# One bank of each visit of maxima goes to ScalarE, and most of those banks hold the difference of two key blocks

## The chip, the cores and the metric

The kernel runs on one core of a Trainium2 chip. The metric is the device time of one execution in microseconds. Besides the times of several runs there is one execution recorded by the hardware profiler. Its engines are called PE (TensorE matmul) and PEld (its weight loads), DVE (VectorE), ACT (ScalarE), POOL (GpSimd) and SP (SyncE, which issues the transfers).

## The reference

Two attentions over the same 2048 tokens of width 448 (16 heads of 28) are mixed with a gate per token. Branch A is linear attention on learned features; branch B is plain softmax attention.

```python
g = _sigmoid((x * gate_w).sum(-1, keepdims=True))
a = _A_ref(x, A_wqkv, A_w_phi, A_wo)
b = _B_ref(x, B_wqkv, B_wo)
return g * a + (1 - g) * b
# in _B_ref
scores = jnp.einsum("bhqd,bhkd->bhqk", q, k) * scale
p = _softmax(scores, axis=-1)
o = jnp.einsum("bhqk,bhkd->bhqd", p, v)
```

The softmax of branch B subtracts the largest score of each query and head. The kernel finds those largest scores in a pass of its own, and this pass is what the change is about.

## The kernel before

**Names.** Heads are taken four at a time: `g` is one of four groups of heads. Queries are taken 512 at a time (`qb`, four blocks), and `gq` counts the 16 pairs of group and query block. Keys are taken 512 at a time where maxima are sought (`kb`, four blocks) and 128 at a time where probabilities are computed (`kt`, 16 tiles).

**Stages.** The front stage projects queries and keys and writes them to HBM (`qkd`), runs branch A, and projects the values. Between its matmuls it already seeks maxima for the first query blocks in 76 units (`mx_unit`, lines 242 to 279). A unit does two heads at once: half of its rows hold the difference of two key blocks. ScalarE takes the relu of that difference (line 270), and VectorE adds it to the score of the other block and takes the maximum in the same instruction (line 272); max(a, b) = b + relu(a - b).

**The late stage** is one loop over 256 steps (lines 1063 to 1101). Step `s` belongs to one `gq` and one key tile `kt`, so 16 steps make one `gq`. Each step does, in this order:

- `scores(s, 0)` and `scores(s, 1)`: four matmuls, one for each head, into four PSUM banks (`st`, line 821), and for each bank an exp on ScalarE into an SBUF tile (`p`, line 839).
- `values(s - 1)`: the probabilities of the step before times the values, into one bank held for the whole `gq` (`pv`, line 947).
- Once in 16 steps `finish`: `pv` is copied out, 384 columns by VectorE and then 128 by ScalarE (line 369). Normalization follows in the next steps, with transfers of the denominators (lines 372, 383, 384), a product on GpSimd (line 390) and a cast on ScalarE (line 398).
- `mx_visit` (lines 287 to 312) in the first 180 steps: the maxima of one tile of 128 queries against one key block for the four heads of a group. Four matmuls that work on 28 rows each go to four banks (`pm`, line 302), and VectorE reduces each bank to a column of `part` (line 306). When a `gq` is finished, `mx_reduce` reduces its columns, negates and transposes them into `nm`, from which the maxima are loaded later as a row of the queries (line 807). The visits run well ahead of the steps that need them: they begin with the last query tile of `gq` 4 in step 1.

**Order.** PE, DVE, ACT and POOL run their instructions in the order in which this program writes them. For SP a scheduler decides the order. The order of the visits is the list `flats`: key block outermost, then query tile.

**Banks.** Seven PSUM banks, `g0` to `g6`, are handed around by the lists `free`, `used` and `held`; the eighth is `pv`. In a step the four scores take four banks, and the visit takes four: the banks of its first and second score of this step and two that the last visit used. The first bank of a visit goes back to `free` at once (line 888), and the next step's fourth score takes it. That score must wait until the bank has been read. The fourth bank of a visit is taken by the third score two steps later.

**Loads.** `mx_load` (line 180) brings the keys of four heads, one block, into a tile `kc` with one transfer per head; there are five such buffers. `mx_query` brings the queries (`qc`). When the group changes (twice in the late stage), the tiles of the next group are loaded as the blocks of the old one are used for the last time (line 307).

Of the kernel before, what the change touches and what calls it, by code (L numbers as in the profile page):

```python
# [8 lines left out]
F32 = mybir.dt.float32  # L9
# [30 lines left out]
def gated_mix_kernel(ctx, tc, xT, wqkB, wvB, wvA, wkAT, wqAT, phi, woA, woB,  # L40
# [116 lines left out]
    acts = []  # L157
    subs = []
    part = mxp.tile([P, NU * 4], F32, name="part", bufs=1)
    neg = mxp.tile([P, 32], F32R, name="neg", bufs=1)  # L160
    nc.vector.memset(f32(neg), 0.0)

# [8 lines left out]
    def mx_rows(r, rows, src, heads, c):  # L171

        for i, j in zip(rows, heads):
            nc.sync.dma_start(f32(r[32 * i:32 * i + DH]), src[DH * j:DH * j + DH, 0, c:c + 512])
        return r

    def mx_tile(tag, nm, bufs):
        return mxp.tile([P, 512], F32R, tag=tag, name=nm, bufs=bufs)

    def mx_load(g, c):  # L180
        mxs[("kc", g, c)] = mx_rows(mx_tile("kc", f"kc{g}_{c}", 5), range(4), k_d[g], range(4),
                                    c * 512)

    def mx_query(gq):
        g, qb = divmod(gq, NQ)
# [2 lines left out]
    def pair_load(g, c):  # L188

        hp, b = divmod(c, 2)  # L190
        heads = (2 * hp, 2 * hp + 1)
        r = mx_tile("kc", f"kp{g}_{c}", 5)
        t = front.tile([P, 512], F32R, tag="kt", name=f"kt{g}_{c}", bufs=1)
        mx_rows(r, (0, 1), k_d[g], heads, b * 1024)
        mx_rows(r, (2, 3), k_d[g], heads, b * 1024 + 512)
        mx_rows(t, (2, 3), k_d[g], heads, b * 1024)
        mxs[("kp", g, c)] = r

        def sub():
            for i in (2, 3):  # L200
                js = slice(32 * i, 32 * i + DH)
                nc.gpsimd.tensor_sub(r[js], f32(r[js]), f32(t[js]))

        subs.append(sub)
# [37 lines left out]
    def mx_unit():  # L242

        u = mxs["u"]
        if u == NF:
            return
        mx_fin()
        mxs["u"] = u + 1
        gq, r = divmod(u, 16)
        g, qb = divmod(gq, NQ)  # L250
        if gq < GM:
            c, qt = divmod(r, 4)
            hp, b = divmod(c, 2)
            col = 64 * gq + 16 * b + 4 * qt + 2 * hp
            if r in (4, 9):
                pair_query(gq + 1, r // 9)
        else:
            c, qt = divmod(r, QM)
            hp, b = divmod(c, 2)
            col = 64 * gq + 4 * QM * b + 4 * qt + 2 * hp  # L260
            if r == 0:
                mx_query(gq)
        qc, kc = mxs[("qp", gq, hp)], mxs[("kp", g, c)]
        pb, pd = ps_mx(f"pmb{u}", False), ps_mx(f"pmd{u}", True)
        for j in range(4):
            js = slice(32 * j, 32 * j + DH)
            nc.tensor.matmul((pb if j < 2 else pd)[:, j % 2, :], qc[js, qt * P:(qt + 1) * P],  # L267
                             kc[js, :], start=True, stop=True, tile_position=(32 * j, 0))
        rl = rlp.tile([P, 2, 512], F32, tag="rl", name=f"rl{u}", bufs=2 if psn[1] == 3 else 1)
        nc.scalar.activation(rl, pd, AF.Relu)  # L270
        for i in range(2):
            nc.vector.tensor_tensor_reduce(rl[:, i, :], pb[:, i, :], rl[:, i, :], 1.0, LOWEST,  # L272
                                           ALU.add, ALU.max, part[:, col + i:col + i + 1])
        if gq < GM and qt == 3 and qb == NQ - 1:
            pair_load(g + 1, c)
        if gq == GM and qt == QM - 1:
            mx_load(g, c)
        if r == 15:
            mx_reduce(gq)


    flats = [(GM, kb, qt, h, 64 * GM + 8 * QM + 4 * (4 - QM) * kb + 4 * (qt - QM) + h)
             for kb in range(4) for qt in range(QM, 4) for h in range(4)]
    flats += [(gq, kb, qt, h, 64 * gq + 16 * kb + 4 * qt + h) for gq in range(GM + 1, NG * NQ)
              for kb in range(4) for qt in range(4) for h in range(4)]

    def mx_visit():

        fins = mxs["fin"][:]
        mxs["fin"].clear()  # L290
        f = mxs["f"]
        todo = flats[f:f + 4]
        mxs["f"] = f + len(todo)
        if todo:
            gq, kb, qt, _, col = todo[0]
            g, qb = divmod(gq, NQ)
            if kb == 1 and qt in (0, QM) and gq + 1 < NG * NQ and ("qc", gq + 1) not in mxs:
                mx_query(gq + 1)
            pm = mx_banks(f)
            for j in range(4):  # L300
                js = slice(32 * j, 32 * j + DH)
                nc.tensor.matmul(pm[j], mxs[("qc", gq)][js, qt * P:(qt + 1) * P],  # L302
                                 mxs[("kc", g, kb)][js, :], start=True, stop=True,
                                 tile_position=(32 * j, 0))
            for j in range(4):
                nc.vector.tensor_reduce(part[:, col + j:col + j + 1], pm[j], AX.X, ALU.max)  # L306
            if qt == 3 and qb == NQ - 1 and g + 1 < NG:
                mx_load(g + 1, kb)
            if qt == 3 and kb == 3:
                mx_reduce(gq)  # L310
        for fn in fins:
            fn()
# [502 lines left out]
    def scores(s, i):  # L815

        gq, kt = divmod(s, NT)
        g, qb = divmod(gq, NQ)

        def score(j, st):  # L820
            nc.tensor.matmul(st, kst_of[(g, kt // 4)][:, j, (kt % 4) * P:(kt % 4 + 1) * P],  # L821
                             qst_of[gq][:, j, :], start=True, stop=True)

        if s == 0:
            p = at.tile([P, 2, 512], F32, name=f"p{s}_{i}")
            st = ps_mx(f"st{s}_{i}", i)
            for jl in range(2):
                score(2 * i + jl, st[:, jl, :])
            nc.scalar.activation(p, st, AF.Exp, scale=SCALE)
            pts.setdefault(s, []).extend([p[:, 0, :], p[:, 1, :]])  # L830
            return
        sts = []
        for j in (2 * i, 2 * i + 1):
            used.append(free.pop(0))
            sts.append(bank(used[-1], f"st{s}_{j}"))
            score(j, sts[-1])
        for st in sts:
            p = late_p.tile([P, 512], F32, tag="p", name=f"p{s}_{len(pts.get(s, []))}", bufs=12)
            nc.scalar.activation(p, st, AF.Exp, scale=SCALE)  # L839
# [330 lines left out]
```

## Time and profile before

| | us |
|---|---|
| median of 3 runs | 1059.6 |
| lowest and highest | 1058.47 to 1061.05 |
| the profiled execution, whole | 1062.47 |
| its span in the trace | 1060.4 |
| visits: first and last maxima matmul | 364.2 to 853.9 |

The profile has several views. The page gives busy time for each engine and 40 equal slices of the span, in which each digit is the busy share in tenths. The view by stretches repeats the busy time for chosen parts, with the number of instructions in brackets. The view by lines groups instructions: busy time, mean duration of one in nanoseconds, and idle time ahead of them with its cause. For one line it gives counts with shortest, median and longest duration. The view in order of time gives start, duration, engine, line, operation, tiles and count, and in square brackets the idle time of the engine just before, with what ended it; several instructions of one kind in a row are merged. The list of waits gives who waited for whom: total, times, longest. The chain of waits follows the work that ended last back from its end.

### The profile page before, as it was taken

Reading aid. Unit: us, or ns where it says so; the run is one execution under the profiler, and the core shown is the slowest. Engines: PE = TensorE matmul, PEld = TensorE weight load, DVE = VectorE, ACT = ScalarE, POOL = GpSimd, SP = SyncE. Lnnn points to the kernel's source line nnn. Section 1 sums busy time; section 2 is a strip of 40 time slices with the busy share of each in tenths; the row PEclk is TensorE's granted clock in tenths of the full one; section 3 lists DMA queues with packets and bytes.
Section 4 is the critical chain, followed back from the end, with each engine's and each line's share of the span. In section 5 each row is a group of like instructions: output and inputs, shape, how many; then the busy total and the mean of one; then the engine's idle time right before and its main releaser. Section 6 shows DMA issues by size and latency. Waiting matters only on the chain.

```text
span 1060.4 us, 17608 instructions
## 1 busy us (share of the span) xinstructions
PE 1046.2 (99%) x6344; PEld 559.5 (53%) x6344; DVE 727.2 (69%) x1351; ACT 756.3 (71%) x1388; POOL 227.8 (21%) x189
## 2 busy tenths in 40 slices
PE   8999999999999999999999999999999999999998
PEld 7777777778777633333333333333333333353545
DVE  5476677897745699999999999999999930000102
ACT  5455565587755777877777777777777798969682
POOL 1234454688536400110000000000000000000000
PEclk9999999999999999999999999999999999999999
DMA  8973100122333822223441233442242234405311
GB/s 290 300 227 96 50 30 30 41 79 78 95 109 100 183 57 55 62 59 84 107 95 48 58 76 97 127 103 60 52 99 50 53 83 96 118 32 149 101 58 53
DMA packets 64190, 99.08 MB, mean 93 GB/s; under 512 B 18008, under 2 KB 24776, under 8 KB 64104
## 3 DMA queue, kind: packets, MB, share of 16 engines
q1 hardware_dynamic: 64104, 97.97, 33.8%
q8 instruction: 50, 0.82, 0.3%
q14 instruction: 36, 0.29, 0.1%
HBM read 69.77 MB, written 27.78 MB: 92 GB/s over the span
## 4 chain that ended last, share of the span: by engine, by line
PE 87%; DVE 7%; DMA 2%; ACT 1%; SPq 1%; issue 1%; POOL 0%; ACTq 0%; DVEq 0%; POOLq 0%
PE st L821 26%; PE pv L947 21%; PE pm L302 7%; PE pqk L108 6%; PE pk L126 4%; PE poa L108 3%; PE pva L126 3%; DVE part L306 3%; PE pob L108 3%; PE pmb L267 3%; PE pq L108 2%; PE pvb L126 2%; PE pvb L108 1%; PE pn L503 1%; PE pqk L605 1%; DMA kst<-qkd 1%
## 5 line engine op out<-in xcount | busy, mean ns | idle before, releaser
L839 ACT ACTIVATE p<-st 128x512 f32<-128x512 f32 x1020 | 526.0, 607 | 137.9 <-PE st L821 134.7
L306 DVE TENSOR_REDUCE part<-pm 128x1 f32<-128x512 f32 x720 | 446.7, 683 | 36.1 <-PE pm L302 35.4
L821 PE MATMUL st<-qst,kst 128*128 128x512 f32 x1024 | 334.7, 439 | 5.0 <-DMA qst<-nm 1.9
L947 PE MATMUL pv<-p,vb 128*32 128x512 f32 x2048 | 273.4, 606 | 0.0
L821 PEld LDWEIGHTS st<-qst,kst 128*128 128x128 f32 x1024 | 173.7, 188 | 175.5 <-DVE part L306 61.7
L272 DVE CUSTOM_DVE_ANT_0 rl<-pmb,rl 128x512 f32<-128x512 f32 x152 | 98.2, 684 | 53.9 <-ACT rl L270 53.9
L390 POOL TENSOR_TENSOR oUb<-oUb,rsb 128x512 f32<-128x512 f32 x15 | 19.3, 1285 | 518.3 <-DMA rsb<-rdb 240.9
L302 PEld LDWEIGHTS pm<-kc,qc 28*128 28x128 f32 x720 | 34.4, 181 | 150.9 <-ACT p L839 150.1
L270 ACT ACTIVATE rl<-pmd 128x1024 f32<-128x1024 f32 x76 | 78.1, 1028 | 39.2 <-PE pmd L267 31.3
L302 PE MATMUL pm<-kc,qc 28*128 28x512 f32 x720 | 90.9, 495 | 0.0
L947 PEld LDWEIGHTS pv<-p,vb 128*32 128x32 f32 x2048 | 40.3, 108 | 72.1 <-issue 66.9
L958 DVE SCALAR_TENSOR_TENSOR acc<-pob,gate,acc 128x448 f32<-128x448 f32 x12 | 8.2, 684 | 94.4 <-PE pob L108 94.4
L108 PE MATMUL pqk<-XH,wB 128*128 128x512 f32 x192 | 59.6, 397 | 1.4 <-DVE ev L543 1.4
L369 DVE COPY oUb<-pv 128x384 f32<-128x384 f32 x15 | 8.3, 551 | 68.9 <-PE pv L947 68.9
L108 PE MATMUL poa<-woA_s,oTa 128*128 128x448 f32 x192 | 43.4, 375 | 0.0
L542 ACT CAST ev<-pqk 128x512 fp32r<-128x512 f32 x28 | 16.0, 588 | 35.5 <-PE pqk L108 34.4
L108 PEld LDWEIGHTS pqk<-XH,wB 128*128 128x128 f32 x192 | 35.3, 188 | 10.2 <-DVE ev L543 1.8
L126 PE MATMUL pk<-wkA_s,XH 128*128 128x448 f32 x128 | 39.4, 381 | 0.0
L267 PE MATMUL pmd<-kp,qp 28*128 28x512 f32 x152 | 37.9, 494 | 1.3 <-DVE part L272 1.3
L108 PEld LDWEIGHTS poa<-woA_s,oTa 128*128 128x128 f32 x192 | 34.9, 188 | 6.3 <-issue 3.3
L267 PE MATMUL pmb<-kp,qp 28*128 28x512 f32 x152 | 38.0, 496 | 0.0
L126 PE MATMUL pva<-wvA_s,XH 128*128 128x450 f32 x128 | 37.8, 371 | 0.0
(151 smaller groups left out, 1102.7 us busy)
## 6 DMA issues: line engine op xcount, KB each, us to landing
qkd<-ev SPq DMA_DIRECT2D x28, 512.0 KB
qst<-qkd SPq DMA_DIRECT2D x64, 224.0 KB
kst<-qkd SPq DMA_DIRECT2D x64, 224.0 KB
od<-oTb SPq DMA_DIRECT2D x48, 112.0 KB
rsa<-rda SPq DMA_DIRECT2D x8, 512.0 KB
rsb<-rdb SPq DMA_DIRECT2D x15, 256.0 KB
gad<-ga SPq DMA_DIRECT2D x16, 224.0 KB
acc<-gad SPq DMA_DIRECT2D x4, 896.0 KB
```

The lines of the kernel that those rows point to most:

```text
L108: nc.tensor.matmul(dst, l, r, start=i == 0, stop=i == len(todo) - 1)
L126: nc.tensor.matmul(dst[:, :n], l, r, start=i == 0, stop=i == len(todo) - 1, skip_group_check=True)
L267: nc.tensor.matmul((pb if j < 2 else pd)[:, j % 2, :], qc[js, qt * P:(qt + 1) * P], kc[js, :], start=True, stop=True, tile_position=(32 * ...
L270: nc.scalar.activation(rl, pd, AF.Relu)
L272: nc.vector.tensor_tensor_reduce(rl[:, i, :], pb[:, i, :], rl[:, i, :], 1.0, LOWEST, ALU.add, ALU.max, part[:, col + i:col + i + 1])
L302: nc.tensor.matmul(pm[j], mxs[("qc", gq)][js, qt * P:(qt + 1) * P], mxs[("kc", g, kb)][js, :], start=True, stop=True, tile_position=(32 * ...
L306: nc.vector.tensor_reduce(part[:, col + j:col + j + 1], pm[j], AX.X, ALU.max)
L390: (nc.gpsimd if n == 1 else nc.vector).tensor_mul(oU, oU, rs)
L542: nc.scalar.copy(e[:, 0, :], pq)
L821: nc.tensor.matmul(st, kst_of[(g, kt // 4)][:, j, (kt % 4) * P:(kt % 4 + 1) * P], qst_of[gq][:, j, :], start=True, stop=True)
L839: nc.scalar.activation(p, st, AF.Exp, scale=SCALE)
L947: nc.tensor.matmul(pv[32 * j:32 * j + 32, :], vb[kt // 8][:, kt % 8, 4 * g + j, :], pt[j], start=kt == 0, stop=kt == NT - 1, tile_position ...
```

## The change

In the late stage one of the four banks of each visit is read by ScalarE instead of VectorE. In visit `kb` this is the bank of head `kb`, and it is the first one: its matmul is issued first and it lies in the bank that goes to the next step's fourth score.

For heads 0, 1 and 2 that bank holds a difference: the tile of keys for block `c` has, in the rows of head `c`, the keys of block `c + 1` less those of block `c`, and in the rows of head `c - 1` those of block `c - 1`. GpSimd makes the difference (`diffs`, three subtractions per group, with the subtrahends in a further tile `kd`; `take_diffs` queues each subtraction two visits after its load was issued). ScalarE writes the relu of the difference into a tile `rl`. In the next visit VectorE adds it to the bank that holds block `c` of that head and takes the maximum in one instruction, as the units do. For head 3 in visit 3 ScalarE copies the bank, and VectorE reduces the copy at the end of the next visit. So four visits have nine reductions of banks, three joins and one reduction of a copy, where they had sixteen reductions. `part` is first filled with a very low number, since some of its columns stay unwritten.

With it go: key blocks innermost in the order of visits; loads of the next group's tiles in the last five visits of the old group; nine buffers of `p` instead of twelve; `kt`, a tile of the front stage, in the place of `kd`.

```diff
+    nc.gpsimd.memset(part, LOWEST)
...
     def mx_load(g, c):
+        mxs[("kc", g, c)] = r = mx_tile("kc", f"kc{g}_{c}", 5)
+        if c == 0:
+            mxs["kd"] = mx_tile("kd", f"kd{g}", 1)
+            for h in range(3):
+                mx_rows(mxs["kd"], (h,), k_d[g], (h,), h * 512)
+        for h in range(4):
+            mx_rows(r, (h,), k_d[g], (h,), 512 * (c + (c == h and c < 3) - (c == h + 1 and c > 0)))
+        if c < 3:
+            js, t = slice(32 * c, 32 * c + DH), mxs["kd"]
+            diffs.append((mxs["u"] + mxs["f"] // 4, lambda: nc.gpsimd.tensor_sub(
+                r[js], f32(r[js]), f32(t[js]))))
+
+    def take_diffs(n):
+        while diffs and diffs[0][0] + n <= mxs["u"] + mxs["f"] // 4:
+            diffs.pop(0)[1]()
...
-             for kb in range(4) for qt in range(QM, 4) for h in range(4)]
+             for qt in range(QM, 4) for kb in range(4) for h in range(4)]
...
     def mx_visit():
+        take_diffs(2)
...
-            pm = mx_banks(f)
-            for j in range(4):
+            pm = mx_banks(f, kb)
+            for j in sorted(range(4), key=lambda j: j != kb):
...
-            for j in range(4):
-                nc.vector.tensor_reduce(part[:, col + j:col + j + 1], pm[j], AX.X, ALU.max)
-            if qt == 3 and qb == NQ - 1 and g + 1 < NG:
-                mx_load(g + 1, kb)
+            rl = late_p.tile([P, 512], F32, tag="rl", name=f"rl{f}", bufs=2)
+            nc.scalar.activation(rl, pm[kb], AF.Relu if kb < 3 else AF.Copy)
+            for j in sorted({0, 1, 2, 3} - {kb}, key=lambda j: j == kb - 1):
+                if j == kb - 1:
+                    r = mxs["rl"]
+                    nc.vector.tensor_tensor_reduce(r, pm[j], r, 1.0, LOWEST, ALU.add, ALU.max,
+                                                   part[:, col + j:col + j + 1])
+                else:
+                    nc.vector.tensor_reduce(part[:, col + j:col + j + 1], pm[j], AX.X, ALU.max)
+            mxs["rl"] = rl
+            if kb == 3:
+                mxs["fin"].append(lambda: nc.vector.tensor_reduce(
+                    part[:, col + 3:col + 4], rl, AX.X, ALU.max))
+            if qb == NQ - 1 and g + 1 < NG:
+                if qt == 2 and kb == 3:
+                    mx_load(g + 1, 0)
+                if qt == 3 and kb < 3:
+                    mx_load(g + 1, kb + 1)
...
-    def mx_banks(f):
+    def mx_banks(f, first):
         b = [free.pop(0) for _ in range(4)]
         free.append(b[0])
         held.extend(b[1:])
-        return [bank(i, f"pm{f}_{j}") for j, i in enumerate(b)]
+        order = [first] + sorted({0, 1, 2, 3} - {first}, key=lambda j: j == first - 1)
+        return [bank(b[order.index(j)], f"pm{f}_{j}") for j in range(4)]
```

More of the change, by code (lines that the diff above doesn't have):

```diff
@@ L178, in mx_tile @@
         return mxp.tile([P, 512], F32R, tag=tag, name=nm, bufs=bufs)
+    diffs = []
     def mx_load(g, c):
-        mxs[("kc", g, c)] = mx_rows(mx_tile("kc", f"kc{g}_{c}", 5), range(4), k_d[g], range(4),
-                                    c * 512)
+        mxs[("kc", g, c)] = r = mx_tile("kc", f"kc{g}_{c}", 5)
[12 more added lines that the diff above has]
+            diffs.pop(0)[1]()
     def mx_query(gq):
@@ L192, in pair_load @@
         r = mx_tile("kc", f"kp{g}_{c}", 5)
-        t = front.tile([P, 512], F32R, tag="kt", name=f"kt{g}_{c}", bufs=1)
+        t = mx_tile("kd", f"kt{g}_{c}", 1)
         mx_rows(r, (0, 1), k_d[g], heads, b * 1024)
@@ L282, in gated_mix_kernel @@
     flats = [(GM, kb, qt, h, 64 * GM + 8 * QM + 4 * (4 - QM) * kb + 4 * (qt - QM) + h)
-             for kb in range(4) for qt in range(QM, 4) for h in range(4)]
+             for qt in range(QM, 4) for kb in range(4) for h in range(4)]
     flats += [(gq, kb, qt, h, 64 * gq + 16 * kb + 4 * qt + h) for gq in range(GM + 1, NG * NQ)
-              for kb in range(4) for qt in range(4) for h in range(4)]
+              for qt in range(4) for kb in range(4) for h in range(4)]
     def mx_visit():
+        take_diffs(2)
         fins = mxs["fin"][:]
@@ L837, in scores @@
         for st in sts:
-            p = late_p.tile([P, 512], F32, tag="p", name=f"p{s}_{len(pts.get(s, []))}", bufs=12)
+            p = late_p.tile([P, 512], F32, tag="p", name=f"p{s}_{len(pts.get(s, []))}", bufs=9)
             nc.scalar.activation(p, st, AF.Exp, scale=SCALE)
```

## The prediction

> **What bounds the kernel now.** I read the page first: its busy shares, and the slices of VectorE and ScalarE.
>
> ```profile
> span 1060.4 us, 17608 instructions
> PE 1046.2 (99%) x6344; PEld 559.5 (53%) x6344; DVE 727.2 (69%) x1351; ACT 756.3 (71%) x1388; POOL 227.8 (21%) x189
> DVE  5476677897745699999999999999999930000102
> ACT  5455565587755777877777777777777798969682
> ```
>
> TensorE's 99% says little, since a matmul that waits counts as busy. The second row of digits matters: from about 365 to 854 us VectorE is at nine tenths. That is the stage of the 180 visits, and the change acts in it alone. The view by stretches compares it with steps that have no visit:
>
> ```profile
> core 0: us, PE busy (x) PEld busy (x) DVE busy (x) ACT busy (x) POOL busy (x), PEclk, DMA share, GB/s
> 364.00:854.00 490.00, 486.84 (x2872) 182.81 (x2868) 455.21 (x771) 379.10 (x744) 30.84 (x25) 1.00 0.31 76
> 857.00:875.00 18.00, 18.00 (x104) 7.08 (x106) 0.57 (x3) 17.58 (x35) 2.58 (x2) 1.00 0.44 97
> ```
>
> 490 us for 180 steps is 2.72 us a step; VectorE works 455 of them (93%), ScalarE 379 (77%). VectorE is nearly full, but not full, so I asked for one step in order of time:
>
> ```profile
> 651.96 0.50 PE L302 MATMUL pm<-kc,qc 28*128 28x512 f32 x4
> ...
> 652.39 1.36 PE L821 MATMUL st<-qst,kst 128*128 128x512 f32 x4
> ...
> 652.49 2.48 DVE L306 TENSOR_REDUCE part<-pm 128x1 f32<-128x512 f32 x4 [0.22 <-PE pm L302]
> 652.92 2.06 ACT L839 ACTIVATE p<-st 128x512 f32<-128x512 f32 x4 [0.62 <-PE st L821]
> 653.24 0.19 PEld L821 LDWEIGHTS st<-qst,kst 128*128 128x128 f32 x1 [0.33 <-DVE part L306]
> ...
> 653.68 1.06 PE L947 MATMUL pv<-p,vb 128*32 128x512 f32 x8
> ...
> 654.68 0.51 PE L302 MATMUL pm<-kc,qc 28*128 28x512 f32 x4
> ...
> 655.21 1.29 DVE L306 TENSOR_REDUCE part<-pm 128x1 f32<-128x512 f32 x2 [0.23 <-PE pm L302]
> ...
> 655.65 0.60 ACT L839 ACTIVATE p<-st 128x512 f32<-128x512 f32 x1 [0.66 <-PE st L821]
> ```
>
> Here is a ring. The bank of the visit's first maxima is given to the fourth score of the next step. VectorE starts on it at 652.49; the fourth score's weights load at 653.24 (+0.75), pv starts at 653.68 (+0.44), the next maxima at 654.68 (+1.00), VectorE on them at 655.21 (+0.53): 2.72 us, the step. So VectorE's *first* reduction sits in the ring, and the other three do not: VectorE idles 0.22 us a step, and ScalarE idles 0.62 at the very place where the ring passes it. The list of waits counts the ring's wait once a visit, and the steps without visits give TensorE's own pace:
>
> ```profile
> PEld st L821 <- DVE part L306: 61.7, 180, 0.8
> ...
> 873.55 1.19 PE L821 MATMUL st<-qst,kst 128*128 128x512 f32 x4
> ...
> 874.68 1.06 PE L947 MATMUL pv<-p,vb 128*32 128x512 f32 x8
> ```
>
> Unstalled, four scores take 1.13 us to pv, against 1.29 in the visit step. TensorE's floor for a visit step is then 1.13 + 1.00 + 0.43 (maxima to scores, 651.96 to 652.39) = 2.56 us.
>
> **The change, part by part.** *The ring.* The bank that goes to the fourth score is now the one that ScalarE reads. In place of VectorE's first reduction stands one ACTIVATE. The single instructions:
>
> ```profile
> 619.62 0.69 DVE L306 TENSOR_REDUCE part<-pm 128x1 f32<-128x512 f32 x1 [0.23 <-PE pm L302]
> L270 ACT ACTIVATE rl<-pmd 128x1024 f32<-128x1024 f32 x76 | 78.1, 1028 | 39.2 <-PE pmd L267 31.3 <-ACT z_s L456 2.5 <-ACT vb L665 1.7
> L398 ACT CAST oTb<-oUb 128x512 fp32r<-128x512 f32 x15 | 9.6, 642 | 0.0
> ```
>
> The reduction takes 0.69, which leaves 0.06 of the 0.75 for the signal. No relu of 128x512 stands in the trace. Below: half of L270's relu, 0.51. Above: the cast of that size, 0.64, or no better than the reduction, 0.69. I take the ScalarE row that follows an idle engine and reads one bank of the same size, the 0.60 at 655.65, and the same 0.06. The ring loses 0.09: 180 x 0.09 = 16.2 us, or 1.44 per 16 steps. At 0.51 TensorE's floor decides, 2.72 - 2.56 = 0.16 a step, 29 us; at 0.69 nothing is gained here.
>
> *Does ScalarE have room?* It queues the relu behind the step's four exps and ahead of the next four. Four exps take 2.06 with the last at about 0.60, so each starts 0.49 behind the one before; five need 2.43 of the new 2.63. The exps end at 652.92 + 2.06 = 654.98, before the maxima at 655.21; the relu fills the idle 0.62 and the next exp starts behind it (655.21 + 0.49 = 655.70, against 655.65 now). Room is left: 0.20 a step.
>
> *VectorE.* Of four reductions a visit, 13 instructions in four visits remain: nine reductions, three joins, one reduction of a stored bank. A join is what L272 does now, and its accumulator read stands beside the next instruction:
>
> ```profile
> L272 DVE CUSTOM_DVE_ANT_0 rl<-pmb,rl 128x512 f32<-128x512 f32 x152 | 98.2, 684 | 53.9 <-ACT rl L270 53.9
> L272 DVE DVE_READ_ACCUMULATOR2_ANT part<- 128x1 f32 x152 | 12.6, 83 | 0.0
> ```
>
> The visit's work falls from 2.48 to about 1.9 (2.5 in one of four), under the step and out of the ring: its banks are wanted a step later. A relu may overwrite its buffer only when VectorE has read it. In the one visit of four with the stored bank that read ends 2.48 and a signal of 0.06 after the step's maxima came, and the relu wants the buffer at 2.63: nothing, and 0.1 x 45 = 4 us if that read takes 0.2 more.
>
> *What happens once in 16 steps.* Two steps in 16 are long now, because VectorE also copies pv (L369) or reduces the finished columns (L232 to L238):
>
> ```profile
> 581.15 1.50 PE L821 MATMUL st<-qst,kst 128*128 128x512 f32 x4
> ...
> 584.01 1.35 PE L821 MATMUL st<-qst,kst 128*128 128x512 f32 x4
> ...
> 586.72 1.36 PE L821 MATMUL st<-qst,kst 128*128 128x512 f32 x4
> ...
> 597.56 0.96 PE L821 MATMUL st<-qst,kst 128*128 128x512 f32 x3
> ...
> 600.56 1.33 PE L821 MATMUL st<-qst,kst 128*128 128x512 f32 x4
> ```
>
> 2.86 and 3.00 against 2.71: 0.15 + 0.29 = 0.44 per 16 steps, and it goes. What is late next is ScalarE, whose own extra work was free in its 0.62:
>
> ```profile
> 580.95 0.55 DVE L369 COPY oUb<-pv 128x384 f32<-128x384 f32 x1
> ...
> 581.53 0.27 ACT L369 COPY oUb<-pv 128x128 f32<-128x128 f32 x1 [0.48 <-DVE oUb L369]
> 581.69 1.09 ACT L839 ACTIVATE p<-st 128x512 f32<-128x512 f32 x2
> ...
> 603.79 2.07 ACT L839 ACTIVATE p<-st 128x512 f32<-128x512 f32 x4 [0.63 <-PE st L821]
> 605.71 0.64 ACT L398 CAST oTb<-oUb 128x512 fp32r<-128x512 f32 x1
> ...
> 427.31 0.59 ACT L142 CAST woB_s<-woB_raw 128x448 fp32r<-128x448 f32 x1
> ```
>
> The cast holds a place of 0.49, 0.29 more than the room. The copy of pv stands ahead of a relu and waits for VectorE's copy of the same tile. VectorE, idle then, can start when pv ends (653.68 + 1.06 = 654.74, 0.47 before the maxima come): +0.03, its 0.55, +0.03, ScalarE's place of 0.16 make 0.77, so the relu is 0.30 late. Behind that relu stand the exps, and the fourth score waits for it: the whole ring. Together 0.59 per 16 steps. The four woB casts (L142) cost about 0.25 each, once: 1.0.
>
> *Loads and GpSimd.* A changeover to the next four heads now issues seven loads and then four a visit, and GpSimd subtracts three times: nine loads and nine subtractions more in all, plus one memset at the start beside the first loads.
>
> ```profile
> L174 SPq DMA_DIRECT2D kc<-qkd x48: 306/383/742, 337.0 to 671.4; - x48
> L202 POOL TENSOR_TENSOR kp<-kp,kt 28x512 fp32r<-28x512 f32 x16 | 21.1, 1322 | 21.6 <-DMA kt<-qkd 18.6 <-PE poa L108 2.0
> SPq L372 <- ACT p L839: 68.0, 15, 8.4
> 523.96 5.91 DMA kst<-qkd
> ```
>
> The lead falls from 13 visits to five, 13.1 us. In SP's queue the loads stand behind the transfer of denominators (L372) of an earlier step. Four issues (4 x 0.38), a landing of no more than the 5.9 that a transfer four times as large shows, and 1.3 of subtraction make 8.7, on a GpSimd that works 31 of the 490 us. I take nothing; if SP stood 8.4 us (its longest wait for L372), a changeover would be 4 us late, and there are two: 8 in all. The nine buffers of p in place of twelve still outlast the two steps that a tile lives: nothing.
>
> *Sum.* Per 16 steps 1.44 + 0.44 - 0.59 = 1.29; 180/16 = 11.25 times, 14.5; less 1.0: 13.5 us. The profiled execution took 1062.5 (span 1060.4 and 2.1 around it): 1049.0. The median of the runs, 1059.6, lies 2.9 lower: **1046.1 us**.
>
> **The rivals.** *ScalarE becomes the bound: slower.* Place: five ACTIVATEs in a step, with relu and exp in turn. From 2.63/5 = 0.53 us each it sets the step, from 2.72/5 = 0.54 the kernel is slower. If each waited for the end of the one before (0.60 and a signal of 0.06), a step were 3.30: 180 x 0.58 = 104 us, 1164; with only the relu not overlapping, 4 x 0.49 + 0.66 = 2.62, no loss. For it: the room is only 0.20 and its queue is in order. Against it: the 0.49 in the rows above, and a cast that follows an exp 1.92 behind the first of four, in step. The Trainium skill speaks for this rival: "ScalarE: Activation LUTs", section "Rules for kernel authors", sends relu and max to VectorE, and budgets about 0.3 us and 0.83 ns an element for each ACTIVATE, by which 512 columns are an estimated 0.73 us, and five of them in turn 3.6. The 0.60 of the trace is below that budget, and the overlap is not in it.
>
> *The relu is no quicker than the reduction.* At 0.69 the ring stays, the extras change from 0.44 to about 0.59 (ScalarE has 0.09 more room, so nearer 0.45), and the woB casts add 1: 1059 to 1062. For it: the 0.64 of the cast. Against: every ScalarE row that reads one bank after idling.
>
> *TensorE's floor.* 29 us gained in the ring, less the extras: 1034. For it: half of 1.03. Against: a relu half as wide isn't half as long, since the exps of 512 columns take 0.60.
>
> *A load is late.* 8 us at most, 1054.
>
> **How the numbers follow.** Chances: the ring as forecast 0.70 (1038 to 1056, from a relu of 0.56 to 0.64 with and without late loads); the floor, below 1038, 0.08; no quicker relu 0.10, half of it within 0.2% of 1059.6 (about what a measurement of this kernel can tell from no change, 2.1 us), the rest a little on either side; ScalarE as the bound 0.12. The range is 1036 to 1056. Faster: 0.70 + 0.08 + 0.05 = 0.83; same 0.05; slower 0.12.
>
> **What would show it.** Right: visit steps of 2.60 to 2.66, the fourth score's weights waiting for ScalarE's relu and no longer for VectorE; the relu starting about 0.53 behind the maxima; VectorE idle a fifth of the stage or more; long steps where the pv copy and the cast stand. Wrong: exps that start over 0.53 apart, a relu that starts late because the exps are still running, TensorE waiting for kc at visits 53 to 56 and 117 to 120, where the heads change over, or steps beyond 2.72.

## The result and the profile after

| | before | after |
|---|---|---|
| median of 4 runs | 1060.32 | 1048.21 |
| lowest and highest | 1058.47 to 1064.11 | 1047.73 to 1051.24 |
| span of the profiled execution | 1060.4 | 1046.8 |
| visits: first score of step 1 to first score of step 181 | 492.1 | 481.0 |
| median step of these 180 | 2.708 | 2.611 |
| steps 145 to 160 together | 43.72 | 42.50 |

The ratio is 0.9887 with a 95% interval of 0.9854 to 0.9921: about 12 us faster. Of the 13.6 us between the two spans, 11.2 lie in the stage of the visits. Of the rest 0.6 lie ahead of it and 1.8 behind it. Of these 1.8, 1.6 are steps 191 to 193: both kernels wait there for the rows of the maxima (1.86 us before, 1.72 after), and only the kernel before then ran for 3.4 us at a granted clock of 0.50 (TensorE's clock as a share of its full speed). None of this is counted in the stage.

The page of the changed kernel, the span and the slices of VectorE and ScalarE:

```profile
span 1046.8 us, 17857 instructions
...
DVE  5476776897855577777778777878788720010102
ACT  5355555577855799999989999999999999969682
```

The nines of the stage have moved from VectorE's row to ScalarE's. The view by stretches says by how much:

```profile
364.00:842.00 478.00, 473.52 (x2864) 182.94 (x2860) 377.45 (x771) 464.65 (x921) 38.46 (x31) 1.00 0.33 78
```

VectorE works 377 of 478 us (79%), ScalarE 465 (97%). By busy time alone ScalarE would now seem to be the bound. One step of the changed kernel in order of time says that it is not:

```profile
653.32 0.50 PE L323 MATMUL pm<-kc,qc 28*128 28x512 f32 x4
...
653.75 1.25 PE L856 MATMUL st<-qst,kst 128*128 128x512 f32 x4
653.85 0.60 ACT L327 ACTIVATE rl<-pm 128x512 f32<-128x512 f32 x1
653.88 1.88 DVE L334 TENSOR_REDUCE part<-pm 128x1 f32<-128x512 f32 x3 [0.71 <-PE pm L323]
654.35 2.06 ACT L874 ACTIVATE p<-st 128x512 f32<-128x512 f32 x4
654.50 0.19 PEld L856 LDWEIGHTS st<-qst,kst 128*128 128x128 f32 x1 [0.22 <-ACT rl L327]
654.93 0.16 PEld L983 LDWEIGHTS pv<-p,vb 128*32 128x32 f32 x8 [0.24 <-issue]
...
655.93 0.51 PE L323 MATMUL pm<-kc,qc 28*128 28x512 f32 x4
```

It is the ring of the prediction with another reader. The relu starts 0.53 behind the maxima (653.85 - 653.32), the fourth score's weights load 0.65 later, pv starts 0.43 behind them, and the next maxima come 1.00 after that: 2.61. Before, the link to the weights was 0.75, from VectorE's start. The bracket names the new releaser, "ACT rl L327". What the weights of the changed kernel's scores waited for, grouped by cause (total, times; "issue" stands for nothing that the profile shows):

```profile
  issue: 91.9, 223
  ACT rl L327: 45.2, 188
```

In the kernel before, the corresponding row was "DVE part L306: 61.7, 180". The difference of the two rows is 16.5 us, 0.09 for each of 180 visits.

**The long steps.** In the quiet part of the stage three steps in 16 exceed 2.61: s = 1 (mod 16) takes 3.04, s = 10 takes 2.73 and s = 11 takes 2.84. The first, in order of time:

```profile
575.13 1.06 PE L983 MATMUL pv<-p,vb 128*32 128x512 f32 x8
...
576.13 0.51 PE L323 MATMUL pm<-kc,qc 28*128 28x512 f32 x4
576.33 0.56 DVE L404 COPY oUb<-pv 128x384 f32<-128x384 f32 x1 [0.35 <-PE pv L983]
...
576.92 0.27 ACT L404 COPY oUb<-pv 128x128 f32<-128x128 f32 x1 [0.32 <-DVE oUb L404]
577.09 0.60 ACT L327 ACTIVATE rl<-pm 128x512 f32<-128x512 f32 x1
...
577.74 0.19 PEld L856 LDWEIGHTS st<-qst,kst 128*128 128x128 f32 x1 [0.65 <-ACT rl L327]
```

The relu starts 0.96 behind its maxima instead of 0.53, since it stands behind ScalarE's copy, and that copy waits for VectorE's. The other two steps follow the cast (ScalarE in order of time):

```profile
643.08 0.60 ACT L327 ACTIVATE rl<-pm 128x512 f32<-128x512 f32 x1
643.57 0.61 ACT L433 CAST oTb<-oUb 128x512 fp32r<-128x512 f32 x1
644.08 2.06 ACT L874 ACTIVATE p<-st 128x512 f32<-128x512 f32 x4
646.00 0.63 ACT L327 ACTIVATE rl<-pm 128x512 f32<-128x512 f32 x1
```

The exps start a place later, at 1.00 behind the relu instead of 0.50, and there is no gap left on ScalarE until the next relu.

**A wait of TensorE.** Step 63 takes 4.82 us; before it took 3.76. SP's queue in order of time, and then the chain of waits, both of the changed kernel:

```profile
515.92 3.37 SPq L1040 DMA_DIRECT2D od<-oTb  x4
519.39 1.83 SPq L830 DMA_DIRECT2D kst<-qkd  x4
521.26 0.83 SPq L830 DMA_DIRECT2D qst<-qkd  x2
522.14 2.97 SPq L842 DMA_DIRECT2D qst<-nm  x4
```

```profile
524.61 6.68 DMA qst<-nm
...
531.53 1.17 PE st L856 x4
```

The first scores of the next `gq` wait for the maxima in `qst`. These small rows are issued behind output rows and a tile of keys, and the chain puts 6.68 us on them. TensorE was done with the step's maxima at 529.14 and waited 2.15 us until the rows had landed. In the kernel before it waited 1.0 us at this place, for the keys' tile (`kst`).

### The profile page after: what moved, and what is told of

It is laid out like the page before. It is cut to its first block, busy times and chain, and to the rows that moved or that the text cites. A ratio compares the mean times of both kernels' runs of the same rounds, so it can differ in the third digit from the quotient of the medians.

```text
span 1046.8 us, 17857 instructions
## 1 busy us (share of the span) xinstructions
PE 1030.3 (98%) x6344; PEld 558.5 (53%) x6344; DVE 650.3 (62%) x1351; ACT 843.2 (81%) x1568; POOL 240.5 (23%) x199
## 4 chain that ended last, share of the span: by engine, by line
PE 89%; DVE 4%; DMA 3%; ACT 2%; SPq 1%; issue 1%; POOL 0%; DVEq 0%; ACTq 0%
PE st L856 26%; PE pv L983 23%; PE pm L323 7%; PE pqk L108 5%; PE poa L108 4%; PE pk L126 4%; PE pva L126 3%; PE pmb L286 3%; PE pob L108 3%; PE pq L108 2%; PE pvb L126 2%; PE pvb L108 2%; DMA qst<-nm 1%; PE pn L538 1%; PE pft L526 1%; DVE featq L453 1%
## 5 line engine op out<-in xcount | busy, mean ns | idle before, releaser
L856 PE MATMUL st<-qst,kst 128*128 128x512 f32 x1024 | 319.4, 429 | 6.2 <-DMA qst<-nm 3.9
L334 DVE TENSOR_REDUCE part<-pm 128x1 f32<-128x512 f32 x405 | 258.2, 684 | 97.1 <-PE pm L323 92.6
L327 ACT ACTIVATE rl<-pm 128x512 f32<-128x512 f32 x180 | 108.4, 602 | 8.0
L331 DVE CUSTOM_DVE_ANT_0 rl<-pm,rl 128x512 f32<-128x512 f32 x135 | 91.8, 680 | 0.0
L108 PEld LDWEIGHTS pqk<-XH,wB 128*128 128x128 f32 x192 | 35.3, 188 | 11.6 <-DVE ev L578 3.2
```

Source lines behind the costliest of these rows:

```text
L108: nc.tensor.matmul(dst, l, r, start=i == 0, stop=i == len(todo) - 1)
L327: nc.scalar.activation(rl, pm[kb], AF.Relu if kb < 3 else AF.Copy)
L331: nc.vector.tensor_tensor_reduce(r, pm[j], r, 1.0, LOWEST, ALU.add, ALU.max, part[:, col + j:col + j + 1])
```

## The experiments

All times are medians; every ratio is against the kernel before on the same chip, with its 95% interval. The columns on steps are read from the trace of one execution. The kernel before took 1060.3 to 1061.9 us beside the several kernels, so small differences between them are read from the stage and not from the medians.

| kernel | median us | ratio | stage of visits | regular step | steps 145 to 160 | 63 and 64 | 127 and 128 |
|---|---|---|---|---|---|---|---|
| changed kernel | 1048.21 | 0.9887 (0.9854 to 0.9921) | 481.0 | 2.61 | 42.50 | 7.35 | 5.30 |
| `e1_ring_only` | 1049.37 | 0.9892 (0.9875 to 0.9910) | 480.4 | 2.61 | 42.65 | 5.48 | 5.46 |
| `e2_off_ring` | 1065.49 | 1.0043 (1.0028 to 1.0058) | 495.5 | 2.70 | 43.97 | 6.68 | 5.41 |
| `e3_pv_copy` | 1045.63 | 0.9857 (0.9837 to 0.9876) | 476.8 | 2.61 | 42.09 | 6.96 | 5.56 |
| `e4_cast` | 1051.13 | 0.9905 (0.9883 to 0.9926) | 485.3 | 2.61 | 42.16 | 10.90 | 9.81 |
| `e5_scalar_free` | 1047.22 | 0.9863 (0.9842 to 0.9883) | 479.5 | 2.61 | 41.77 | 11.09 | 9.33 |
| `e9_rows_only` | 1045.38 | 0.9841 (0.9825 to 0.9857) | 478.7 | 2.61 | 42.49 | 5.21 | 5.22 |
| `e6_early_rows` | 1035.27 | 0.9747 (0.9732 to 0.9762) | 469.6 | 2.61 | 41.77 | 5.22 | 5.22 |
| `e10_ring_full` | 1035.88 | 0.9748 (0.9731 to 0.9766) | 469.7 | 2.61 | 41.77 | 5.20 | 5.22 |
| `e11_half_read` | 1027.39 | 0.9673 (0.9658 to 0.9688) | 460.9 | 2.56 | 40.99 | 5.12 | 5.12 |
| `e7_room1` | 1057.81 | 0.9958 (0.9943 to 0.9974) | 489.5 | 2.64 | 43.13 | 8.57 | 5.33 |
| `e8_room3` | 1166.16 (one run) | none | 600.3 | 3.29 | 53.34 | 6.58 | 6.58 |
| `e12_split_read` | 1096.71 | 1.0333 (1.0315 to 1.0351) | 531.0 | 2.83 | 47.14 | 6.12 | 6.12 |

### The ring without the differences

```diff
-            nc.scalar.activation(rl, pm[kb], AF.Relu if kb < 3 else AF.Copy)
+            nc.scalar.activation(rl, pm[kb], AF.Copy)
...
-                if j == kb - 1:
-                    r = mxs["rl"]
-                    nc.vector.tensor_tensor_reduce(r, pm[j], r, 1.0, LOWEST, ALU.add, ALU.max,
-                                                   part[:, col + j:col + j + 1])
-                else:
-                    nc.vector.tensor_reduce(part[:, col + j:col + j + 1], pm[j], AX.X, ALU.max)
+                nc.vector.tensor_reduce(part[:, col + j:col + j + 1], pm[j], AX.X, ALU.max)
...
+            mxs["fin"].append(lambda: nc.vector.tensor_reduce(
+                part[:, col + kb:col + kb + 1], rl, AX.X, ALU.max))
```

The loads of keys are those of the kernel before, one transfer for each head and no subtraction, but written where the changed kernel has its loads; there are three buffers of `rl` and eight of `p`.

> One part of the change alone: ScalarE reads the first bank of every visit (a plain copy into a buffer), but there are no differences, no joins and no extra loads; VectorE reduces the copy in the next visit, so it has 16 reductions in four visits, as the kernel before had. Ring theory (the first read of a visit is what the ring waits for, and ScalarE's read is 0.09 us shorter): regular steps of 2.61 to 2.63 us, TensorE's fourth score waits for ScalarE, the whole at 1046 to 1052 us, the upper end if VectorE's own copies make it late once in 16 steps. Rival, VectorE's load (the time fell because VectorE has less to do, 378 of 481 us in place of 456 of 492): VectorE's work is what it was, so steps of about 2.70 and 1057 to 1062 us.

Measured: 1049.37, a regular step of 2.61. The view by stretches, and what the fourth scores waited for:

```profile
364.00:830.00 466.00, 462.35 (x2796) 179.03 (x2792) 440.91 (x751) 453.89 (x899) 30.86 (x25) 1.00 0.33 78
PEld st L840 <- ACT rl L318: 44.2, 178, 0.8
```

VectorE works 441 of 466 us here, 95%, more than in the kernel before, and the time is still that of the changed kernel. So the gain doesn't come from VectorE's relief.

### The same work, with VectorE in the ring

```diff
+    def visit_order(kb):
+        x, *rest = sorted({0, 1, 2, 3} - {kb}, key=lambda j: j == kb - 1)
+        return [x, kb] + rest
...
-            for j in sorted(range(4), key=lambda j: j != kb):
+            for j in visit_order(kb):
...
-        order = [first] + sorted({0, 1, 2, 3} - {first}, key=lambda j: j == first - 1)
+        order = visit_order(first)
```

> The same operations on every engine as in the changed kernel, differences, joins and loads included; only the order within a visit differs: VectorE reads the first bank of a visit, the one that the next step's fourth score takes, and ScalarE's bank is the second. Ring theory: the ring has VectorE's 0.69 in it again, steps of 2.69 to 2.72 us, the whole at 1057 to 1064 us (less what ScalarE's long steps no longer cost, since its cast and copy are out of the ring: down to 1054). Rival, VectorE's load: VectorE has as little to do as in the changed kernel, so 2.61 us steps and 1047 to 1050 us.

Measured: 1065.49, slower than the kernel before and 1.5 us above the range. The two rows, as in the last experiment:

```profile
364.00:830.00 466.00, 461.40 (x2708) 172.60 (x2704) 356.65 (x729) 438.19 (x871) 38.08 (x31) 1.00 0.33 77
PEld st L856 <- DVE part L334: 56.6, 165, 0.9
```

VectorE has only 357 us to do, and the step is 2.70 again. These two runs are the pair to look at: much work on VectorE and a fast step, little work and a slow one. What decides between them is the reader of the first bank. The loss against the kernel before lies mainly in three steps of 16: s = 7, where the finished columns are reduced, takes 3.11 in place of 3.00, and s = 10 and 11, with ScalarE's cast, take 2.76 and 2.81 in place of 2.70 and 2.71. Without the ring the change only costs.

### ScalarE's copy of pv

```diff
-            else:
-                c = slice(384 * i, 384 + 128 * i)
-                (nc.scalar.copy if i else nc.vector.tensor_copy)(oU[:, 0, c], pn[0][:, c])
+            elif i == 0:
+                nc.vector.tensor_copy(oU[:, 0, :], pn[0])
```

> VectorE copies all 512 columns of pv; ScalarE's 128 are gone. If the long step s = 1 (mod 16), 3.04 against 2.61 us, is long because the relu stands behind ScalarE's copy, which stands behind VectorE's: that step falls to 2.61 to 2.70 us, 0.34 to 0.43 less in 11 steps, 3.7 to 4.7 us, so 1043 to 1045 us. Rival, pv itself is late (its bank must be emptied before the next head group's first pv, whoever does it): the step stays near 3.0, and the whole within 1 us of 1048.

Measured: 1045.63, 0.6 us above the range. The stage is 4.2 us shorter and s = 1 (mod 16) takes 2.61, as expected. VectorE's copy of 512 columns takes 0.69, but the relu no longer waits for it:

```profile
575.61 0.51 PE L323 MATMUL pm<-kc,qc 28*128 28x512 f32 x4
575.81 0.69 DVE L403 COPY oUb<-pv 128x512 f32<-128x512 f32 x1 [0.35 <-PE pv L982]
...
576.14 0.60 ACT L327 ACTIVATE rl<-pm 128x512 f32<-128x512 f32 x1
```

The relu is 0.53 behind its maxima again. The copy was the cause.

### ScalarE's cast

```diff
-            nc.scalar.copy(oT[:, 0, :], oU[:, k, :])
+            (nc.vector.tensor_copy if n == 1 else nc.scalar.copy)(oT[:, 0, :], oU[:, k, :])
```

> The cast of the normalized values once in 16 steps (128 x 512) is done by VectorE in place of ScalarE. If the steps s = 10 and 11 (mod 16), 2.73 and 2.84 us in place of 2.61, are long because ScalarE's room of 0.19 us a step doesn't hold the cast's place of 0.49: 0.34 less in 11 groups of 16 steps, 3.7 us, 1044 to 1045 us. Rival, VectorE takes the loss over (its cast of 512 columns, about 0.6, stands ahead of the reads of a visit): the steps stay long, 1047 to 1049 us.

Measured: 1051.13, in neither range. The quiet steps did what was expected: 2.62 and 2.60 at s = 10 and 11, 0.34 less per 16 steps. But steps 63, 64, 127 and 128 together took 20.7 us instead of 12.7. The chain of waits, then the view by stretches for step 64 and for step 128:

```profile
525.21 6.42 DMA qst<-nm
...
531.87 2.05 PE st L856 x4
```

```profile
531.90:536.40 4.50, 4.50 (x16) 1.59 (x16) 0.55 (x1) 2.06 (x4) 0.00 (x0) 0.50 0.45 90
704.80:709.30 4.50, 4.50 (x16) 1.57 (x16) 0.56 (x1) 2.06 (x4) 0.00 (x0) 0.50 0.37 74
```

The rows land at 531.63 (525.21 + 6.42), about when they did (531.29), but TensorE stands ready earlier (at 527.98 instead of 529.14) and the output rows are issued later (at 516.84 instead of 515.92), so it waits 3.65 us (the 4.16 of the next text counts from the start of the last maxima, not from their end). Then comes a second loss: the column behind the counts is the granted clock, and it is 0.50 through the step that follows. The experiment on the cast had run into the loads; the next three runs separate the two.

### All of ScalarE's extras, the loads, and both

`e5_scalar_free` has both edits above and gives VectorE the four woB casts too. `e9_rows_only` is the changed kernel with the loads moved, and `e6_early_rows` has everything.

```diff
-            if kt == 12 and gq + 1 < NG * NQ:
+            if kt == (6 if gq + 1 < 14 else 12) and gq + 1 < NG * NQ:
                 load_q(gq + 1)
-            if kt == (12 if gq + 1 < 14 else 14) and gq + 1 < NG * NQ - 1:
+            if kt == (6 if gq + 1 < 14 else 14) and gq + 1 < NG * NQ - 1:
                 load_nm(gq + 1)
```

> VectorE takes all three of ScalarE's extras: the copy of pv, the cast once in 16 steps and the four woB casts. If their costs are what the long steps showed one by one (0.43 and 0.34 per 16 steps, 0.3 for each woB cast), 16 quiet steps take 41.7 to 41.9 us in place of 42.50 and no step is long but the two at the loads of the next queries' rows (steps 63 and 64, 127 and 128). These loads are not moved, and in the run with the cast on VectorE TensorE waited there 4.16 and 3.08 us and then ran a step at a granted clock of 0.50, some 5.7 and 4.6 us more than a regular step and its successor take beyond the changed kernel's: so the whole is 1044 to 1048 us, though by the steps alone it would be 1038.6. Rival, VectorE becomes late (1.1 us more in 16 steps stand ahead of its reads): 16 quiet steps stay at 42.1 or more.

> The changed kernel with one thing else: the loads of the next block of queries and of their maxima are written six steps earlier, ahead of the output rows and of the keys' tile in SP's queue. If TensorE's wait at steps 63 and 127 (4.82 and 2.77 us in place of 2.61) is those small rows landing 6.7 us after their issue behind large transfers, both steps fall to 2.61 to 2.7 us, 2.3 us less, 1045 to 1047 us. Rival, the wait goes to the keys' tile that is then the last to land (the kernel before waited 1.06 us for it): step 63 stays above 3.6.

> ScalarE's three extras on VectorE, and the loads of the queries and their maxima six steps earlier. If the extras' costs and the wait for the rows add, nothing is left in the stage of the visits but steps of 2.61 us, 16 quiet steps at 41.8, and the whole at 1034 to 1038 us. Rival, the rows only hide the next wait: 1040 us or more.

Measured: 1047.22, 1045.38 and 1035.27, each in its range. Without the extras 16 steps take 41.77, which is 16 regular ones, and with the loads moved steps 63 and 127 take 2.61. In the stage the extras alone bring 1.4 us beside the changed kernel, the loads alone 2.3, both together 11.3: without the loads moved, the time that ScalarE gives back is spent waiting for the rows and, in steps 64 and 128, at a lowered clock. In `e9_rows_only` step 191, behind the stage, falls as well, from 3.90 to 2.12. The stage of 469.6 us is 180 times 2.609, so nothing but the ring is left in it. It is the fastest whole computation tried.

### What the differences buy

`e10_ring_full` is `e6_early_rows` with plain copies in place of the differences, the edit of the first experiment.

> Plain copies in place of differences (16 reductions of 512 columns on VectorE in four visits, no joins, no extra loads of keys), with ScalarE's three extras on VectorE and the rows loaded six steps earlier. It tells what the differences are worth where VectorE has the extras. VectorE's work in 16 steps is then 64 reductions of about 0.62 us, a copy of 0.57, a cast of about 0.6 and the columns' 0.30: 41.2 of 41.8 us. If only the ring counts, steps of 2.61 and 1034 to 1038 us, as with differences. Rival, VectorE has become the next bound: steps that are long where its extras stand, 0.5 to 1.5 us per 16 steps more, 1041 to 1053 us.

Measured: 1035.88, beside 1035.27 with the differences; the steps are equal. A stretch of 40 us, first without and then with them:

```profile
580.00:620.00 40.00, 40.00 (x246) 15.59 (x249) 39.13 (x69) 39.16 (x78) 2.57 (x2) 1.00 0.31 74
```

```profile
580.00:620.00 40.00, 40.00 (x244) 15.78 (x243) 33.01 (x67) 39.21 (x78) 2.57 (x2) 1.00 0.30 73
```

VectorE goes from 33 to 39 of 40 us and nothing gets longer. The differences, most of the change's text, take 15% of the stretch off an engine that had the time. Before the extras are moved they bring little: 16 quiet steps take 42.65 without them and 42.50 with them, by the step s = 1 (3.13 on average in `e1_ring_only`). Its stage is no longer for it, since its step 63 is shorter (2.96 for 4.82); why was not followed up.

### TensorE's floor

```diff
-            nc.scalar.activation(rl, pm[kb], AF.Relu if kb < 3 else AF.Copy)
+            nc.scalar.activation(rl[:, :256], pm[kb][:, :256], AF.Relu if kb < 3 else AF.Copy)
```

The join and the reduction of the stored bank read the same 256 columns.

> The kernel with ScalarE's extras on VectorE and the early rows, but ScalarE and the join read 256 of the bank's 512 columns; the maxima leave the other half of that bank out. The ring's read is then about 0.2 us shorter. If TensorE's own work is the floor that the prediction worked out, 2.56 us a step, steps go from 2.61 to 2.56 and no further: 180 x 0.05 = 9 us, 1024 to 1029 us. Rival, something else of 2.61 us stands beside the ring: no change, 1034 to 1037. Rival, no floor at 2.56: steps below 2.54 and less than 1022.

Measured: a step of 2.56 and 1027.39. The groups of relu and join:

```profile
L327 ACT ACTIVATE rl<-pm 128x256 f32<-128x256 f32 x15 | 5.8, 384 | 0.8
L331 DVE CUSTOM_DVE_ANT_0 rl<-pm,rl 128x256 f32<-128x256 f32 x12 | 5.0, 415 | 0.0
```

The relu is 0.22 shorter (384 against 602 ns), the step only 0.05. The list of what the scores' weights waited for has no relu any more ("ACT rl" stood there with 39.2 us, 180 times, in `e6_early_rows`): TensorE's own work ends the step, at the 2.56 that the prediction had worked out.

### ScalarE's room

One and three copies that nobody reads, behind each relu of the changed kernel:

```diff
             nc.scalar.activation(rl, pm[kb], AF.Relu if kb < 3 else AF.Copy)
+            for _ in range(1):
+                nc.scalar.copy(idle, ident)
```

> One more instruction on ScalarE in each visit, a copy of 128x128 that nobody reads, behind the relu: a place of about 0.16 us in its queue. If ScalarE has the 0.20 us a step that five places of 0.48 leave in 2.61, regular steps stay at 2.61 to 2.63; the steps that the cast and the copy of pv make long grow, since the room that took up a part of them is gone (up to 0.2 + 0.2 + 0.2 per 16 steps, 7 us): 1049 to 1056 us. If ScalarE already sets the step (the rival of the prediction), each copy adds its 0.16: 180 x 0.16 = 29 us, 1077.

> The changed kernel with three copies of 128x128 in each visit that nobody reads, in place of the one tried before. With one, steps were 2.64 us and ScalarE's exps followed one another without a gap. If ScalarE sets the step from there on, the two further copies add their place of 0.19 each: 2.64 + 0.38 = 3.02 us, 180 x 0.38 = 68 us more than with one, 1120 to 1130 us. Rival, the 2.64 came from something else, such as a later relu: about 2.7 us a step, 1070.

Measured: 1057.81 and 1166.16, 1.8 and 36 us above their ranges. With one copy the steps are 2.64. ScalarE in order of time, in the first kernel and then in the second:

```profile
592.85 0.62 ACT L328 ACTIVATE rl<-pm 128x512 f32<-128x512 f32 x1
593.35 0.30 ACT L330 COPY idle<-ident 128x128 f32<-128x128 f32 x1
593.53 2.09 ACT L877 ACTIVATE p<-st 128x512 f32<-128x512 f32 x4
595.48 0.63 ACT L328 ACTIVATE rl<-pm 128x512 f32<-128x512 f32 x1
```

```profile
594.83 0.62 ACT L328 ACTIVATE rl<-pm 128x512 f32<-128x512 f32 x1
595.31 0.99 ACT L330 COPY idle<-ident 128x128 f32<-128x128 f32 x3
596.21 2.05 ACT L877 ACTIVATE p<-st 128x512 f32<-128x512 f32 x4
598.12 0.62 ACT L328 ACTIVATE rl<-pm 128x512 f32<-128x512 f32 x1
```

The copy's place, from its start to the next one's, is 593.53 - 593.35 = 0.18 to 0.19, the five others take 2.45 of 2.64, and there is no gap. So the changed kernel's room was 2.61 - 2.45 = 0.16, and the copy exceeds it by 0.03. That is 5 us over 180 steps; the step s = 10, now 2.94 instead of 2.73, adds 2, and step 64 ran 1.6 us longer at a granted clock of 0.56, which the expectation did not have. With three copies the step is 0.65 longer, not 0.38: each copy starts only when the one before has ended, 0.33 apart, three in 0.99. That all of them write one buffer may be the reason; it was not tried. The expected mechanism, ScalarE setting the step, holds; the price of a copy had been taken from one with an exp behind it.

### The floor with a whole computation

```diff
-            nc.scalar.activation(rl, pm[kb], AF.Relu if kb < 3 else AF.Copy)
+            nc.scalar.activation(rl[:, :384], pm[kb][:, :384], AF.Relu if kb < 3 else AF.Copy)
+            if kb < 3:
+                nc.vector.tensor_scalar_max(rl[:, 384:], pm[kb][:, 384:], 0.0)
+            else:
+                nc.vector.tensor_copy(rl[:, 384:], pm[kb][:, 384:])
```

> A whole computation at the floor, if there is one: the kernel with ScalarE's extras on VectorE and the early rows, and the first bank of a visit read by two engines, 384 columns by ScalarE and 128 by VectorE, which does them first in its visit. ScalarE's read is then about 0.49 us (between 0.60 for 512 columns and 0.38 for 256), which leaves the ring at TensorE's floor of 2.56. VectorE has about 0.25 us more in a visit, 2.40 of 2.56 us. If VectorE is always done with the visit before when the new maxima come: steps of 2.56, 1025 to 1030 us. Rival, VectorE comes late to its slice behind the stored bank's reduction in one visit of four, and the ring waits for it as it did in the kernel before: those steps longer than 2.61, and the whole at 1033 us or more.

Measured: 1096.71. That is in the rival's range, but two thirds of the loss have a cause that neither text has. In order of time:

```profile
593.61 0.51 PE L323 MATMUL pm<-kc,qc 28*128 28x512 f32 x4
...
594.13 0.49 ACT L327 ACTIVATE rl<-pm 128x384 f32<-128x384 f32 x1 [0.38 <-PE pm L323]
...
594.66 0.29 DVE L329 TENSOR_SCALAR rl<-pm 128x128 f32<-128x128 f32 x1 [0.73 <-ACT rl L327]
...
595.00 0.19 PEld L859 LDWEIGHTS st<-qst,kst 128*128 128x128 f32 x1 [0.43 <-DVE rl L329]
```

VectorE is idle and begins 0.04 after ScalarE has ended. The two reads stand in series, 0.49 + 0.04 + 0.29, and the ring is longer than either kernel's: three steps of four take 2.83. The fourth takes 3.29, and there it is, as in the rival, VectorE's reduction of the stored bank that comes late:

```profile
602.09 0.51 PE L323 MATMUL pm<-kc,qc 28*128 28x512 f32 x4
602.32 0.68 DVE L341 TENSOR_REDUCE part<-rl 128x1 f32<-128x512 f32 x1
...
603.09 0.49 ACT L327 ACTIVATE rl<-pm 128x384 f32<-128x384 f32 x1 [0.79 <-PE st L859]
```

What waits is the relu, 1.00 behind its maxima. The bracket names the scores, but in each such visit the relu begins 0.09 after that reduction has ended; it writes the buffer that the reduction reads, since `rl` has two. Over `e6_early_rows` the series costs 0.22 in each of 180 steps, 40 us, and this wait 0.46 in each of 45, 20 us. In the changed kernel too the relu of every fourth visit mostly begins 0.10 after the reduction, yet at its regular 0.53 behind the maxima: the wait costs nothing there, but it has next to nothing to spare. As for the series, both reads write the tile `rl` and read one bank; which of the two makes VectorE wait was not tried, so whether a whole computation can reach 2.56 stays open.

## Why the prediction was right, point by point

- **The ring: right.** 0.09 a step were forecast, 0.097 measured; the relu takes 602 ns where 0.60 was taken from an exp. Its cause is shown by two runs that move VectorE's load and the ring apart.
- **VectorE's long steps: right.** The 0.44 per 16 steps went. That the differences were needed for it isn't so: the step s = 7 is regular in `e1_ring_only` too.
- **ScalarE's room: a little small.** 0.20 was forecast, and the run with one copy shows 0.16: the step came out 2.61 and not 2.63, and five places take 2.45 and not 2.43. The cast therefore costs 0.34 and not 0.29. The Trainium skill, "ScalarE: Activation LUTs", section "What ACT_TABLE_LOAD costs", lets two ACTIVATEs in a row overlap by about 93 ns, and gives an ACTIVATE without pointer operands 186 ns and 0.833 ns an element. Five places of 512 columns would by that be an estimated 2.60 and leave no room; its 0.61 for one agrees with the trace's 0.60, and the overlap in the trace is larger.
- **The copy of pv: mis-sized.** 0.30 was forecast, 0.43 measured. The term at fault is VectorE's start: 0.03 behind pv's end was taken, and the rows show 576.33 against 575.13 + 1.06 = 576.19, 0.14. The remaining 0.02 is 0.01 each in VectorE's copy (0.56) and in ScalarE's place (577.09 - 576.92 = 0.17).
- **The woB casts:** 1.0 forecast, 1.2 measured (steps 17 to 48 are 1.9 us shorter in `e5_scalar_free` than in `e3_pv_copy`, of which 0.7 is the cast).
- **The loads: the step that failed.** They were costed at nothing, with a bound of 8 us, and only the keys of the visits were looked at. These were in time: no changeover waits for `kc`. What came late were other transfers, which the diff does not touch: the rows of `qst` landed 2.15 us after TensorE was ready for step 64. From the first issue of output rows, which stand ahead of them in SP's queue, until TensorE is ready there are 13.2 us (515.92 to 529.14), and 14.3 in the kernel before (519.46 to 533.72). How much of that is the shorter steps and how much the order in the queue was not separated. Over four steps (63, 64, 127, 128) the excess above regular ones rose from 0.8 to 2.2 us, 1.4 more.
- **The sum.** In the stage: 17.5 from the ring and 4.8 from VectorE's long steps, less 4.7 (copy, 11 times), 3.4 (cast, 10 times), 1.2 and 1.4, is 11.6; measured 11.2; forecast 13.5. Of the forecast's 2.3 too much 1.7 are the extras and 1.4 the loads; the ring brought 1.3 above its forecast, and 0.4 stand in no step that was singled out. That the ring's error took back a part of the others is luck. The whole came out at 1048.2 for 1046.1, within the range; the kernel before stands at 1060.3 with its fourth run, 0.7 above the 1059.6 that the forecast went by.
- **The rivals.** ScalarE does become the bound, but at 0.16 more a step than the change gives it. The relu was quicker than the reduction (602 against 683 ns). TensorE's floor is where it was put, 0.05 below the ring. A late load was real, in another place and smaller than its bound.

## What to carry to other kernels

Where banks circulate, follow one bank round and see who reads it first: the latency of that one read is in every step, while the load of an engine says little by itself: in `e10_ring_full` VectorE and ScalarE both worked 98% of a stretch whose steps were the ring's. Work moved to an engine with little room turns its rare extras into long steps, so move these along, and look again at every transfer that had just been in time. The two edits here, ScalarE's extras moved and the rows loaded earlier, were worth 1.4 and 2.3 us of the stage alone and 11.3 together, so a small result of one edit says little as long as another wait stands ready to take the time back.

## What the runs showed of the hardware

TensorE's granted clock falls after some waits, which costs 1.5 to 2 us more. Waits of 3.65, 3.84 and 2.57 us were each followed by a step at 0.50, which took 4.57 us instead of the changed kernel's 2.53, waits of 2.59 and 1.76 by steps at 0.57 and 0.56 (4.06 and 4.10 us); one of 2.15 in the changed kernel, and one of 1.75 in `e3_pv_copy`, by a full-speed step. The Trainium skill, "TensorE: Matmul & The Clock Gate", section "What's actually happening", puts the half rate after an idle window of about 3.4 us, with windows that run freely. None of these waits fills such a window. The stretches at half rate last 3.41 or 6.83 us; counted in windows of 3.41 us from their edges, the wait of 3.84 us (527.03 to 530.87 in `e5_scalar_free`) lies 1.69 in one window and 2.15 in the next, and the half rate begins between the two, at 528.72. So it matters how a wait falls: the 2.15 us of the changed kernel are 1.24 and 0.91 in two windows and kept the clock, the 1.76 us of `e7_room1` lie in one and lost it. The length in a window is not the whole rule either: 1.77 us in one kept the clock in `e1_ring_only`, at step 192, and 1.74 lost it in `e4_cast`, at step 128.

ScalarE's ACTIVATEs that read one bank each started 0.48 to 0.50 apart though one lasts 0.60, also where relu and exp take turns, and copies into one and the same buffer started 0.33 apart where a copy ahead of an exp takes a place of 0.19.
